# A decode layer on one core: the products with wo as a loop with addresses in registers

## The chip, the core and the metric

The kernel runs on one core of a Trainium2 chip. A core has five engines, each with its own instruction stream: TensorE (PE, matrix products; its weight loads are listed as PEld), VectorE (DVE), ScalarE (ACT), GpSimd (POOL) and SyncE (SP). [...] Engines work on SBUF, an on-chip memory of 128 partitions; TensorE writes its results to PSUM, another one. DMA engines move data between HBM and SBUF. Engines wait for each other by semaphores. The metric is the device time of one execution in microseconds.

## What is computed

One step of a decoder layer for four sequences (B = 4, D = 576): layernorm, attention over the last 4096 positions of a cache with 16 key/value heads and 32 query heads of 128, then layernorm and a gated MLP with F = 4608, each with a residual. Cut to what matters:

```python
W = min(4096, max(256, Sk // 4))
q = (x @ wq).reshape(B, Sq, Hq, Dh).transpose(0, 2, 1, 3)
k = jnp.repeat(k_cache[:, :, Sk - W:, :], rep, axis=1)
v = jnp.repeat(v_cache[:, :, Sk - W:, :], rep, axis=1)
p = softmax(einsum("bhqd,bhkd->bhqk", q, k) * Dh ** -0.5)
o = einsum("bhqk,bhkd->bhqd", p, v)
attn = o.transpose(0, 2, 1, 3).reshape(B, Sq, Hq * Dh) @ wo      # 4096 x 576
h = x + attn
hn = layernorm(h)
gate = relu(hn @ W_gate); up = hn @ W_up
out = h + (gate * up) @ W_down
```

## The kernel before

The cache is read in 16 units ("quads") of four (batch, head) pairs each, one 4 MB transfer for K and one for V per quad, into four slots of the SBUF tensor `pool`. For each quad, DVE transposes K in four pieces (`kT`, line 451), PE multiplies it with the queries (`qk`, line 544), DVE and ACT do the softmax, DVE transposes the probabilities, and PE multiplies them with V (`pv`, line 562). PE's program runs this as a hardware loop of eight turns of two quads (`S.loop`, lines 115 to 147, called at line 593); its head is placed with `head_slot`. Everything else on every engine is unrolled. No register enters an address anywhere: in the loop, registers hold only the values that semaphores are compared with (line 86, 143).

Order within an engine is the order of the code in `prog_pe`, `prog_dve`, `prog_act`, `prog_pool` and `prog_sync`. `Sched` runs these programs twice, once to number the semaphore counts of named operations and once to emit them, and puts in the waits that each operation's `deps` ask for.

After the loop, PE finishes the last quad and, with DVE, scales the attention output (`o_bf`, line 489). Four products with `spread` (line 602) bring it into the layout of `oX`, 128 partitions by EO = 32 groups by 4 sequences, which ACT copies to SBUF (line 395). Then come the products with wo (lines 604 to 610). wo lies in `pool` as 128 partitions by 32 rows of D = 576; for each row `e_`, PE loads `oX[:, e_, :]` as weights (128 x 4) and multiplies the row with it in two halves of HD = 288 columns. All 32 rows add up in the same 4 x 576 of PSUM (`attn`). The second half is a matmul with `held=True` (lines 515 to 518), which uses the weights already loaded.

The last matmul is named ATTN. What waits for it: DVE's `h_row` (line 492), which adds x and begins the second layernorm (lines 493 and 494); and all six transfers of W_down (lines 300 to 304), because they go to the place in `pool` where wo lies. These six stand on SP's queue behind those of W_gate and W_up (lines 293 to 297), which go elsewhere in `pool`, and ahead of the store of the output (line 316). SP issues every large transfer.

After the layernorm PE transposes the result (line 611), ACT copies it to `hnT`, PE forms gate and up (lines 621 to 640), ACT takes the relu, DVE multiplies (line 496) and transposes to `hhT` (line 500), and PE forms the 36 products with W_down, each in two column parts in separate PSUM partitions, `down(0)` and `down(1)` (lines 642 to 651). ACT and DVE copy these to `out_sb` (lines 406 and 503), which SP stores.

## Time and profile before

| | |
|---|---|
| runs, median (lowest to highest) | 377.74 us (377.6 to 378.22), 3 runs |
| profiled execution | 377.95 us |
| its span | 376.6 us |
| mean granted TensorE clock | 0.918 |
| HBM read | 159.58 MB, 424 GB/s over the span |
| busy: PE / DVE / ACT / POOL | 307.4 / 226.6 / 53.4 / 6.1 us |
| 64 matmuls with wo | 343.19 to 353.04 us |
| six W_down transfers | issued from 353.06, last landed at 373.32 us |
| products with W_down | 366.84 to 374.74 us |

The profile is one execution. Times in it are microseconds from the start of the span; the execution's own time is 1.35 us more than the span. Lines such as L513 are lines of the kernel; since a helper records all matmuls, L513 is a matmul that loads its weights and L515 one with held weights, and the names after them say which product it is. A name like `sc<-pool,oX` gives the tile written and the tiles read, without indices. "Idle before, releaser" tells how long the engine stood idle ahead of an instruction and what ended that; "issue" means that nothing in the profile explains the wait. The PE clock column is the share of full clock that was granted.

### The profile page before, as it was taken

To read this page: it belongs to the slowest core of one execution; us is meant where nothing else is said; L and a number is where in the kernel's file an instruction comes from. 1 tells how busy PE (TensorE), PEld (TensorE's weight loads), DVE (VectorE), ACT (ScalarE), POOL (GpSimd) and SP (SyncE) were. 2 spreads that over 40 slices of the span, in tenths; PEclk is the share of its full clock that TensorE was granted. 3 is DMA by queue.
4 is the path that set the end of the run, shared out by engine and by line. 5 is a ranking of instruction groups with operands and counts; after the bars stand their busy time and mean duration, and the time that the engine had idled before them with its cause. 6 is when DMAs were issued, how large, how long until landed. Compare 5 with 4: busy or idle time off the path is not lost.

```text
span 376.6 us, 2757 instructions
## 1 busy us (share of the span) xinstructions
PE 307.4 (82%) x1454; PEld 74.0 (20%) x778; DVE 226.6 (60%) x165; ACT 53.4 (14%) x140; POOL 6.1 (2%) x16
## 2 busy tenths in 40 slices
PE   0439999959995999599959996899679977986677
PEld 0102221212121212022201221122112211222214
DVE  8255849494839492949475758675677658222230
ACT  2231220202020202002200211021102010101020
POOL 6000000000000000000000000000000000000000
PEclk9959999989998999589976999899989998996988
DMA  8999999999999999999999999999999999999995
GB/s 335 445 444 432 404 445 445 425 412 442 442 421 421 442 445 432 407 442 445 432 411 439 445 432 414 435 445 432 414 435 445 432 418 435 433 421 435 442 399 237
DMA packets 6501, 159.66 MB, mean 424 GB/s; under 512 B 728, under 2 KB 864, under 8 KB 1632
## 3 DMA queue, kind: packets, MB, share of 16 engines
q1 hardware_dynamic: 6488, 159.59, 98.8%
q8 instruction: 3, 0.05, 0.1%
q14 instruction: 2, 0.02, 0.0%
q10 hardware_dynamic: 8, 0.00, 0.0%
HBM read 159.58 MB, written 0.00 MB: 424 GB/s over the span
## 4 chain that ended last, share of the span: by engine, by line
DMA 60%; DVE 27%; PE 11%; ACT 1%; SPq 1%; issue 0%; DVEq 0%
DMA pool<-in_A_k_cache_dram 55%; DVE kT L451 20%; DMA pool<-in_B_W_down_dram 5%; DVE acc L468 4%; PE sc L513 3%; PE sc L515 3%; DVE P L465 2%; PE val L513 2%; PE val L515 2%; PE pb L513 1%; DVE o_bf L489 0%; ACT L386 0%; DVE probT L462 0%; DVE rmx L454 0%; ACT P L386 0%
## 5 line engine op out<-in xcount | busy, mean ns | idle before, releaser
L451 DVE STREAM_TRANSPOSE kT<-pool 128x2048 f32<-128x2048 f32 x64 | 142.7, 2279 | 20.2 <-DMA pool<-in_A_k_cache_dram 20.1
L513 PE MATMUL sc<-kT,qz 128*128 128x512 bf16 x256 | 109.2, 426 | 40.3 <-DVE kT L451 40.2
L513 PE MATMUL val<-pool,probT 128*64 128x512 bf16 (+2 forms) x344 | 111.2, 374 | 3.1 <-DMA pool<-in_B_W_down_dram 3.1
L515 PE MATMUL sc<-kT,qz 128*128 128x512 bf16 x256 | 108.3, 423 | 0.0
L515 PE MATMUL val<-pool,probT 128*64 128x512 bf16 x272 | 103.1, 379 | 0.0
L513 PEld LDWEIGHTS sc<-kT,qz 128*128 128x128 bf16 x256 | 26.3, 103 | 149.5 <-DVE kT L451 77.1
L513 PEld LDWEIGHTS val<-pool,probT 128*64 128x64 bf16 (+1 forms) x344 | 34.1, 107 | 89.1 <-issue 77.6
L454 DVE TENSOR_REDUCE rmx<-sc 128x1 f32<-128x1024 f32 x16 | 19.6, 1225 | 38.5 <-PE sc L515 38.5
L381 ACT ACTIVATE diag<-spot,rmx 128x16 f32<-128x16 f32 x16 | 4.9, 307 | 242.5 <-DVE rmx L454 242.5
L462 DVE STREAM_TRANSPOSE probT<-P 128x1024 bf16<-128x1024 bf16 x16 | 19.9, 1245 | 20.5 <-ACT P L386 20.5
L386 ACT ACTIVATE P<-sc,bias 128x1024 bf16<-128x1024 f32 x16 | 17.8, 1115 | 18.7 <-DVE bias L457 18.7
L375 ACT COPY qz<-qrep 32x128 bf16<-32x128 bf16 x64 | 18.8, 293 | 0.6
L457 DVE TENSOR_REDUCE bias<-pb 128x1 f32<-128x16 f32 x16 | 2.8, 175 | 22.0 <-PE pb L513 22.0
L465 DVE TENSOR_TENSOR P<-val,mask 128x1024 f32<-128x1024 f32 x8 | 9.5, 1190 | 10.6 <-PE val L515 10.6
L468 DVE TENSOR_REDUCE acc<-P 128x128 f32<-128x1024 f32 x8 | 15.2, 1898 | 0.3
L513 PE MATMUL sc<-pool,oX 128*4 128x288 bf16 x32 | 9.4, 324 | 0.4 <-ACT oX L395 0.4
L515 PE MATMUL sc<-pool,oX 128*4 128x288 bf16 x32 | 9.4, 324 | 0.0
L525 PE MATMUL pb<-ident_b,xn_bf 4*128 4x4 bf16 (+1 forms) x5 | 0.4, 179 | 10.7 <-DVE xn_bf L419 10.7
L492 DVE TENSOR_TENSOR h_row<-sc,x_bf 4x576 f32<-4x576 f32 x1 | 0.7, 746 | 11.0 <-PE sc L515 11.0
L513 PE MATMUL sc<-col,foe 4*128 4x512 bf16 x16 | 6.3, 397 | 1.2 <-ACT qrep L361 1.2
L513 PEld LDWEIGHTS pb<-diag,same 128*128 128x128 f32 x32 | 4.8, 188 | 10.0 <-ACT diag L381 10.0
L513 PE MATMUL pb<-diag,same 128*128 128x16 f32 x32 | 6.3, 273 | 0.0
(103 smaller groups left out, 79.1 us busy)
## 6 DMA issues: line engine op xcount, KB each, us to landing
pool<-in_A_k_cache_dram SPq DMA_DIRECT2D x16, 4096.0 KB, 27.3
pool<-in_A_v_cache_dram SPq DMA_DIRECT2D x16, 4096.0 KB, 27.3
pool<-in_A_wo_dram SPq DMA_DIRECT2D x1, 4608.0 KB, 18.4
pool<-in_B_W_gate_dram SPq DMA_DIRECT2D x1, 4608.0 KB, 19.9
pool<-in_B_W_up_dram SPq DMA_DIRECT2D x1, 4608.0 KB, 23.2
pool<-in_A_wq_dram SPq DMA_DIRECT2D x1, 4096.0 KB, 12.6
pool<-in_B_W_down_dram SPq DMA_DIRECT2D x1, 2016.0 KB, 13.7
pool<-in_B_W_down_dram SPq DMA_DIRECT2D x1, 1296.0 KB, 16.5
```

The lines of the kernel that those rows point to most:

```text
L375: S.op(a, lambda e, src=src, dst=dst: e.copy(out=dst, in_=src), deps=deps, name=("QZ", i) if g == 3 else None, signal=g == 3, inc=8 if i = ...
L381: S.op(a, lambda e, i=i: e.activation(out=diag[:, i % 2, :], in_=spot[:, :], func=ACT.Copy, scale=rmx[:, i % 2:i % 2 + 1]), deps=[("RMAX", ...
L386: S.op(a, lambda e, i=i: e.activation(out=Pb[:, (i % 2) * 1024:(i % 2 + 1) * 1024], in_=sc[:, (i % 2) * 1024:(i % 2 + 1) * 1024], func=ACT ...
L451: S.op(v, lambda e: e.transpose(out=dst, in_=src), deps=deps, name=("TR", f), inc=3 if f == 5 else 1)
L454: S.op(v, lambda e: e.tensor_reduce(out=rmx[:, i % 2:i % 2 + 1], in_=sc[:, (i % 2) * 1024:(i % 2 + 1) * 1024], axis=AX.X, op=ALU.max), dep ...
L457: S.op(v, lambda e: e.tensor_reduce(out=bias[:, i % 2:i % 2 + 1], in_=pb[TPB][:, 16 * (i % 2):16 * (i % 2) + 16], axis=AX.X, op=ALU.min), ...
L462: S.op(v, lambda e: e.transpose(out=pT[i % NPT], in_=Pb[:, (i % 2) * 1024:(i % 2 + 1) * 1024]), deps=[("EXP", i)] + ([("PV", i - NPT)] if ...
L465: S.op(v, lambda e: e.tensor_tensor(out=own_sb[:, :].rearrange("p (x d) -> p x d", d=DH), in0=val[:, :].rearrange("p (x d) -> p x d", d=DH ...
L468: S.op(v, lambda e: e.tensor_reduce(out=acc[:, w, :], in_=own_sb[:, :].rearrange("p (x d) -> p d x", d=DH), axis=AX.X, op=ALU.add), deps=[ ...
L492: S.op(v, lambda e: e.tensor_tensor(out=h_row[:, :], in0=attn, in1=x_bf[:, :], op=ALU.add), deps=["ATTN", land("x")], name="H")
L513: return e.matmul(o, lhsT=l, rhs=r, start=start, stop=stop, skip_group_check=skip)
L515: return e.add_instruction(mybir.InstMatmult(name=nc.get_next_instruction_name(), start_tensor_calc=start, stop_tensor_calc=stop, bass_ski ...
```

## The change

Rows 1 to 30 of the products with wo become a hardware loop on TensorE of ten turns of three rows. The row's number follows from the loop's counter, and the address of the weights in `oX` and the address of the row in `pool` are computed from it in registers (`bass.ds` with a register as its start). Row 0, which carries the waits, and row 31, which signals ATTN, stay outside with fixed addresses. A new function `Sched.repeat` makes the loop; unlike `Sched.loop` it gives no `head_slot`, and no wait in it depends on the counter. The products, their order and their places are the same. The other engines' programs are the same.

```diff
+    def repeat(self, eng, n, body):
+        if not self.emit:
+            for i in range(n):
+                body(i)
+            return
+        count = self.counters[eng]
+        with self.engines[eng].Fori(0, n) as i:
+            body(i)
+        assert self.counters[eng] == count
...
-            for e_ in range(EO):
-                deps = [land(("wo",)), "OX"] if e_ == 0 else []
+            def wo_row(e_, first, last):
+                deps = [land(("wo",)), "OX"] if first else []
                 for u in range(2):
-                    c0 = at[("wo",)] + e_ * D + u * HD
-                    mm(attn[:, u * HD:(u + 1) * HD], oX[:, e_, :], pool[:, c0:c0 + HD], e_ == 0, e_ == EO - 1,
-                       deps=deps, name="ATTN" if e_ == EO - 1 and u == 1 else None, held=u == 1)
+                    mm(attn[:, u * HD:(u + 1) * HD], oXf[:, bass.ds(e_ * B, B)], pool[:, bass.ds(e_ * D + at[("wo",)] + u * HD, HD)], first, last,
+                       deps=deps, name="ATTN" if last and u == 1 else None, held=u == 1)
                     deps = []
+
+            oXf = oX[:, :, :].rearrange("p e b -> p (e b)")
+            wo_row(0, True, False)
+            S.repeat(t, (EO - 2) // 3, lambda i: [wo_row(i * 3 + 1 + k, False, False) for k in range(3)])
+            wo_row(EO - 1, False, True)
```

In the built kernel a turn of this loop holds, on PE: seven fused register instructions (33 register operations), three single register additions, one compare-and-branch, three weight loads and six matmuls.

## The prediction

> **What bounds the kernel now.** I read the chain of waits first, over the last 25 us, because the change touches only work that lies there. Columns are start, duration, what.

> ```profile
> 352.90 0.14 PE sc L515
> 353.04 0.02 issue
> 353.06 0.33 SPq L303
> ...
> 354.38 18.94 DMA pool<-in_B_W_down_dram
> 373.32 0.04 issue
> 373.36 0.70 PE val L513 x7
> ...
> 374.78 0.42 DVE out_sb L503
> ```

> The last product with wo ends at 353.04. Two things wait for it: SP, which then issues the six W_down transfers (L303), and DVE's h_row (L492), behind which stand the second layernorm, the gate and up products, and the products with W_down. The chain goes by the transfers, but the other branch is close behind. Next come the stages, by busy time in windows (length, then busy time and count by engine, TensorE clock, DMA share, GB/s).

> ```profile
> 343.00:347.00 4.00, 3.81 (x17) 1.10 (x9) 0.00 (x0) 1.32 (x2) 0.00 (x0) 0.50 0.96 409
> 347.00:353.10 6.10, 6.03 (x49) 1.96 (x23) 0.04 (x1) 0.00 (x0) 0.00 (x0) 1.00 1.12 481
> 361.00:366.80 5.80, 3.36 (x71) 0.61 (x24) 2.68 (x5) 2.06 (x3) 0.00 (x0) 1.00 0.98 410
> 366.80:374.80 8.00, 7.30 (x72) 4.32 (x72) 0.27 (x2) 0.02 (x1) 0.00 (x0) 0.79 0.73 299
> ```

> In the wo stage (the first two rows) PE is busy without a gap, first at half clock, then at full. In the last row it is busy for 7.30 of 8.00 us while W_down still arrives: the down stage waits for data now and then, and has little room. Third, the timeline of one wo row, late in the stage:

> ```profile
> 352.50 0.09 PEld L513 LDWEIGHTS sc<-pool,oX 128*4 128x4 bf16 x1 [0.16 <-issue]
> 352.62 0.29 PE L513 MATMUL sc<-pool,oX 128*4 128x288 bf16 x1
> 352.74 0.29 PE L515 MATMUL sc<-pool,oX 128*4 128x288 bf16 x1
> ```

> A row costs 0.24 us at full clock (two starts 0.12 apart), 0.48 at half. Last, TensorE's sequencer, in the records of the lines that make its first loop and its waits (count: shortest/median/longest ns, first and last start):

> ```profile
> L139 PEldq MOVE  x9: 37/37/39, 20.2 to 285.5; - x9
> L139 PEldq COMPARE_BRANCH  x9: 76/208/309, 20.3 to 323.4; - x9
> L139 PEldq ALU_OP  x8: 32/32/32, 53.8 to 323.3; - x8
> L86 PEldq ALU_OP  x88: 32/32/42, 20.7 to 318.8; - x88
> ```

> **The change, part by part.** Rows 0 and 31 stay as they are. Removed are the 90 plain instructions of rows 1 to 30 (a weight load and two matmuls each), which PE executed in about 9.1 us and which cost the sequencer nearly nothing. In their place the built kernel's order of instructions has one turn, run ten times, of: seven fused register instructions holding 33 register operations in all, two single additions, the counter's addition, a compare-and-branch, three weight loads and six matmuls that take an address from a register. No wait, transfer or buffer changes on any engine.

> Now the turn, in the sequencer:
> - three single additions x 97 ns = 0.29 us;
> - the back-edge, 0.27 us;
> - seven fused instructions. The trace has none. From below, each costs at least one ALU_OP: 7 x 97 = 0.68. From above, its 33 operations cost as much as apart: 33 x 97 = 3.20. The nearest row is the ALU_OP, 32 ns of it work and 65 around it; if the 65 are paid once per instruction, 7 x 65 + 33 x 32 ns = 1.51. I take the middle of 0.68 and 1.51, 1.10;
> - nine loads and matmuls with an address in a register. From below, like the matmul with a wait on a register: 15 ns each, 0.14 (as low as 0.07 if that matmul is no dearer than 8 ns, the 120 ns from MOVE to ALU_OP less 97, over three). From above, like a DMA issue on SP with its addresses (L303, 432 ns median): 3.9. I take 97 ns, 0.87, since fetching a register is what an ALU_OP does.

> Turn T = 0.29 + 0.27 + 1.10 + 0.87 = 2.53 us. PE's own work in it is 0.73 us at full and 1.44 at half clock, so it is covered by the sequencer: the engine waits for its instructions. [...]

> The stage: row 0 starts at 343.19 as before, while the sequencer goes on to MOVE and the entry branch (0.47 us, under row 0's 0.48), so the first turn starts at 343.65. Ten turns, less 0.17 for the last branch, plus 0.54 for row 31 (352.50 to 353.04): the stage ends at 344.0 + 10T = 369.3, which is 16.3 later than 353.04.

> What that delays. SP's queue holds the six W_down issues behind this one wait, then only the output's store. The earlier wg and wu transfers land by about 361.8 (issued at 337.26 and 337.74, 23.2 and 24.1 us to landing), so the DMA engines then idle until about 369.4. The 5.3 MB that follow take some 12.7 us at 410 GB/s, plus some 2 us to start: all landed by about 384. The other branch, h_row to hhT, is a fixed string of DVE, ACT and PE work and moves as a whole: the down products, whose hhT was ready by the semaphore wait at 366.43 and which began at 366.84 only when the first W_down piece came, may begin at 366.5 + 16.3 = 382.8, long after that piece. So W_down, now ending the chain, no longer does; hhT does.

> That gives a little back. A down row's matmuls start 136 ns apart at full clock and 267 at half. With the 3.41 us of half clock that this stage had, 36 rows without waits take 12.8 x 0.267 + 23.2 x 0.136 + 0.3 for the end = 6.9 us: from 366.5 to 373.4, where the trace ends at 374.74. So -1.3 us (-3.0 if all at full clock, +1.7 if all at half).

> Sum against the profiled execution, 377.95 (span 376.6): 377.95 + 16.3 - 1.3 = **392.9 us**; for any turn, 367.6 + 10T. The median of the runs is 377.74, 0.2 below the profiled one, less than what is uncertain here.

> **Rivals.**
> - Cheap addresses: a matmul with a register's address passes like the one with a register's wait. T = 0.29 + 0.27 + 1.10 + 0.14 = 1.80, 385.6; with every bound low, 1.31, 380.7. For it: 15 matmuls and loads in 15 ns. Against: there the register held a wait, not an address.
> - Dear register operations: 33 x 97 ns. T = 0.29 + 0.27 + 3.20 + 0.87 = 4.63, 413.9 (with addresses as dear as a DMA issue instead, T = 5.55, 423.1). Against: they are fused into seven instructions.
> - Not slower: the sequencer's work hides under PE's. This needs 10T below 9.0 + 1.3, so T below 1.03, or ten register instructions at 76 ns or less. It decides only if fused instructions cost about what ALU_OP's busy time says (32 ns): T = 10 x 0.032 + 0.27 + 0.07 = 0.66, all hidden, some 377.7. Against it: no register operation in PE's sequencer is followed by its next control instruction in less than 96 ns.
> - The code is fetched anew at each back-edge. The instruction queue's 16 KB packets took 1.0 to 1.1 us each; nine of them add at least 9.9: 402.8. Against: seven taken back-edges of a body eleven times as long took 207 to 233 ns. [...]
> - The clock stays at half after a loop of sparse matmuls, in place of the mix of before: the up stage's 2.6 us of matmuls double, and the down stage goes to +1.7. That is 2.6 + 3.0 us on top: 398.5. Against: the K loop of before, whose PE also waits, is mostly at full clock.

> **How the numbers follow.** The forecast (388 to 398.5, the clock's rival at its edge) gets 0.51, cheap addresses (380.5 to 388) 0.25, dear register operations or addresses (398.5 and above) 0.15, refetching 0.04, not slower 0.05. The range 382 to 405 leaves out not slower, the lowest bounds of cheap addresses (0.04), and the upper half of the dear case (0.08). A change of 0.2% (0.76 us) can be told from none; not slower splits into same 0.03 and faster 0.02, the other cases are slower, 0.95.

> **What would show it.** In the changed kernel PE has idle time ended by issue in the wo stage, some 1.1 to 1.8 us a turn, and the sequencer's records follow each other without a gap: fused ones at about 160 ns of pitch, matmuls at about 97 each. The stage ends near 369. DMA has an idle stretch from 362 to about 370, and the chain at the end goes by PE and DVE from the stage to the output, with no W_down transfer. Wrong would be: turns of under 1.03 us, wo matmuls still back to back, or a W_down transfer still in the chain.

## The result, and the profile after

The changed kernel takes 382.92 us (median of 4 runs, 381.82 to 383.84) against 377.86 (4 runs, 377.6 to 378.22): a ratio of 1.0132, 95% interval 1.0104 to 1.0161. It is slower, by 5.1 us where 15 were forecast, and 382.92 lies in the range, at its low edge. The profiled execution took 382.82 us with a span of 381.5.

Where the time went, from the two traces (us):

| | before | after | later by |
|---|---|---|---|
| first matmul with wo | 343.19 | 343.75 | 0.57 |
| last matmul with wo ends | 353.03 | 359.47 | 6.44 |
| the wo stage | 9.84 | 15.72 | 5.88 |
| first half of hhT ready | 366.39 | 372.76 | 6.37 |
| products with W_down begin | 366.84 | 372.91 | 6.06 |
| products with W_down end | 374.74 | 379.63 | 4.89 |
| span | 376.6 | 381.5 | 4.9 |

The first 0.57 us come from ahead of the change, in work that is the same in both kernels (see e2 and e3 on what moves it); the stage itself grew by 5.88, the string of work behind it moved along, and the last stage gave some of it back. The chain of waits over the end of the changed kernel (start, duration, what):

```profile
359.35 0.14 PE sc L525
359.48 0.02 issue
359.51 0.76 DVE h_row L502
...
361.87 0.58 DVE hn_row L429
...
368.17 0.28 PE pb L523 x4
...
371.98 0.79 DVE probT L510
372.77 0.14 issue
372.90 6.75 PE val L523 x46
379.65 0.02 issue
379.68 0.42 DVE out_sb L513
```

No transfer is left in it. The products with W_down start 0.14 us after DVE's transpose to hhT and run without a break; SP's issues of W_down, now at 359.5, are no part of it. Busy time in windows (length; busy time and count of PE, PEld, DVE, ACT, POOL; PE clock; DMA share; GB/s), for the wo stage, the stretch to hhT and the products with W_down, first of the kernel before, then of the changed one:

```profile
343.10:353.10 10.00, 9.84 (x64) 3.05 (x32) 0.04 (x1) 1.24 (x1) 0.00 (x0) 0.81 1.06 453
353.10:366.80 13.70, 8.06 (x130) 1.91 (x50) 5.11 (x11) 3.10 (x8) 0.00 (x0) 0.88 0.95 402
366.80:374.80 8.00, 7.30 (x72) 4.32 (x72) 0.27 (x2) 0.02 (x1) 0.00 (x0) 0.79 0.73 299
```

```profile
343.70:359.50 15.80, 13.70 (x64) 2.60 (x32) 0.00 (x0) 1.21 (x1) 0.00 (x0) 0.81 0.96 412
359.50:372.90 13.40, 7.99 (x130) 1.83 (x51) 4.87 (x11) 3.10 (x8) 0.00 (x0) 0.87 0.97 391
372.90:379.70 6.80, 6.72 (x72) 4.04 (x72) 0.54 (x2) 0.03 (x1) 0.00 (x0) 0.75 0.15 53
```

In the first row of the changed kernel PE is idle for 2.1 us, and its busy time is padded by matmuls that no longer overlap: 13.70 us for the 64 matmuls that took 9.84 before, though one is as long as then (282 to 448 ns against 286 to 444). In the last the DMA share is 0.15, against 0.73 before: nearly all of W_down is there when the products start, and its last transfer, landing at 375.90, is ahead of the rows that need it. Now one turn of the loop at full clock, in the timeline:

```profile
351.84 0.08 PEld L523 LDWEIGHTS sc<-pool,oX 128*4 x1 [0.69 <-issue]
351.85 0.28 PE L523 MATMUL sc<-pool,oX 128*4 x1 [0.33 <-issue]
351.98 0.28 PE L525 MATMUL sc<-pool,oX 128*4 x1
352.19 0.08 PEld L523 LDWEIGHTS sc<-pool,oX 128*4 x1 [0.27 <-issue]
352.22 0.28 PE L523 MATMUL sc<-pool,oX 128*4 x1
352.35 0.28 PE L525 MATMUL sc<-pool,oX 128*4 x1
352.60 0.08 PEld L523 LDWEIGHTS sc<-pool,oX 128*4 x1 [0.33 <-issue]
352.63 0.28 PE L523 MATMUL sc<-pool,oX 128*4 x1
352.76 0.28 PE L525 MATMUL sc<-pool,oX 128*4 x1
```

Rows start 0.37 to 0.41 us apart in place of 0.24, the next turn 1.53 us later, and what ends PE's idle time is "issue": no engine and no transfer that the profile shows. What fills these stretches are the records of PE's own sequencer, which the trace lists under PEldq: in the changed kernel 70 FUSED_REGOPS (the fused register instructions), 126 ALU_OP (the single ones), 19 COMPARE_BRANCH and 10 MOVE, and no such record for any other engine. By line (count: shortest/median/longest ns, first and last start):

```profile
L121 PEldq FUSED_REGOPS  x10: 78/78/83, 344.0 to 357.7; - x10
L121 PEldq ALU_OP  x10: 32/32/32, 345.1 to 358.8; - x10
L121 PEldq COMPARE_BRANCH  x10: 76/212/214, 345.2 to 358.9; - x10
...
L528 PEldq FUSED_REGOPS  x30: 55/55/60, 344.2 to 358.7; - x30
...
L523 PEldq FUSED_REGOPS  x30: 51/79/79, 344.1 to 358.5; - x30
L523 PEldq ALU_OP  x20: 32/34/36, 344.5 to 358.6; - x20
```

From the starts in the trace: a fused instruction of 6 operations (78 or 79 ns busy) holds the sequencer for 137 ns, one of 4 (55 or 60) for 113 to 118. The one of 3 (51) is always followed by a weight load and a matmul here and takes 129 with them; alone, in e2 below, it takes 109. Worked out from the 109 and 137 ns for 3 and 6 operations, an estimate is some 81 ns for the instruction and 9.3 for each operation; it gives 118 for 4. Between the fused instruction at 350.339 and the next at 350.457, 118 ns, stands a held matmul with its address in a register: beside the estimated 118 it adds nothing that shows. A weight load with its matmul adds some 20 ns in most turns. Nor is that a price for each: in e6 all nine weight loads and matmuls of a turn stand behind its fused instruction of 3 operations, and this one takes 129 ns again, so the nine together add 20, and at most 70 in the longer of e6's turns. A back-edge takes 271 ns from the branch to the first fused instruction of the next turn.

### The profile page after: what moved, and what is told of

Read it like the earlier page. It is cut to its first block, busy times and chain, and to the rows that moved or that the text cites. A ratio compares the mean times of both kernels' runs of the same rounds, so it can differ in the third digit from the quotient of the medians.

```text
span 381.5 us, 2868 instructions
## 1 busy us (share of the span) xinstructions
PE 311.4 (82%) x1454; PEld 73.3 (19%) x778; DVE 226.9 (59%) x165; ACT 53.4 (14%) x140; POOL 6.1 (2%) x16
## 4 chain that ended last, share of the span: by engine, by line
DMA 54%; DVE 27%; PE 16%; issue 1%; ACT 1%; SPq 0%; DVEq 0%
DMA pool<-in_A_k_cache_dram 54%; DVE kT L461 18%; PE sc L523 5%; PE sc L525 4%; DVE acc L478 4%; PE val L523 4%; DVE P L475 2%; PE val L525 2%; PE pb L523 1%; DVE o_bf L499 0%; ACT L396 0%; DVE probT L472 0%; DVE rmx L464 0%; ACT P L396 0%; PE pb L525 0%
## 5 line engine op out<-in xcount | busy, mean ns | idle before, releaser
L461 DVE STREAM_TRANSPOSE kT<-pool 128x2048 f32<-128x2048 f32 x64 | 142.7, 2279 | 20.4 <-DMA pool<-in_A_k_cache_dram 20.2
L523 PE MATMUL sc<-pool,oX 128*4 (+1 forms) x32 | 10.8, 337 | 2.5 <-issue 2.0
L525 PE MATMUL sc<-pool,oX 128*4 (+1 forms) x32 | 10.9, 341 | 0.0
```

Source lines behind the costliest of these rows:

```text
L461: S.op(v, lambda e: e.transpose(out=dst, in_=src), deps=deps, name=("TR", f), inc=3 if f == 5 else 1)
L523: return e.matmul(o, lhsT=l, rhs=r, start=start, stop=stop, skip_group_check=skip)
L525: return e.add_instruction(mybir.InstMatmult(name=nc.get_next_instruction_name(), start_tensor_calc=start, stop_tensor_calc=stop, bass_ski ...
```

## The experiments

Theory A: the sequencer's register instructions set the pace of the wo stage, and any delay of the stage beyond a little room at the end delays the end. Against it stand, for the pace, the loop itself (B) and the instructions with an address in a register (C); for the end, that W_down goes on setting it (E), or that the loss is in PE's sparse pace (F).

| kernel | turn, us | wo stage, us | median, us | ratio to before, 95% |
|---|---|---|---|---|
| before | none | 9.84 | 377.76 to 377.87 | 1 |
| changed | 1.53 | 15.72 | 382.92 | 1.0104 to 1.0161 |
| a2, changed again | 1.53 | 15.71 | 382.75 | 1.0110 to 1.0139 |
| e1, fixed addresses | 0.73 (PE) | 10.47 | 377.81 | 0.9995 to 1.0020 |
| e2, wo's address only | 1.15 | 11.92 | 380.09 | 1.0042 to 1.0095 |
| e3, weights' address only | 1.16 | 11.95 | 379.03 | 1.0017 to 1.0044 |
| e4, two turns of fifteen | 6.05 | 12.56 | 379.47 | 1.0029 to 1.0060 |
| e5, plain, more rows | none | 16.12 | 382.80 | 1.0102 to 1.0144 |
| e6, addresses together | 1.03 to 1.08 | 11.42 | 377.98 | 1.0001 to 1.0019 |
| e7, six rows a turn | 1.61 to 1.95 | 11.49 | 378.00 | 0.9992 to 1.0011 |

**e1: the loop without registers in addresses.**

```diff
-            S.repeat(t, (EO - 2) // 3, lambda i: [wo_row(i * 3 + 1 + k, False, False) for k in range(3)])
+            S.repeat(t, (EO - 2) // 3, lambda i: [wo_row(1 + k, False, False) for k in range(3)])
```

> The same loop of ten turns, but with the addresses of rows 1 to 3 in every turn, so no register enters an address (rows 4 to 30 are left out of the result, the number of products is the same). Theory A (the sequencer's register work sets the pace): a turn needs 0.10 (counter) + 0.27 (back-edge) us of the sequencer plus some 0.06 for loads and matmuls, less than the 0.73 that PE needs, so the wo stage takes its 9.85 us as in the kernel before and the time is 377.9 +- 0.5. Theory B (the loop itself costs: each back-edge lets PE run dry, or fetches code anew): an idle stretch of 0.3 us or more per turn stays, 379 or more.

377.81 us, not to be told from before. In e1's trace the matmuls follow each other as if unrolled (minimum/median/maximum ns, first and last start):

```profile
L523 PE MATMUL sc<-pool,oX x32: 286/286/448, 344.1 to 354.1; 128*4 128x288 bf16 x32
L525 PE MATMUL sc<-pool,oX x32: 286/286/448, 344.3 to 354.2; 128*4 128x288 bf16 x32
```

The first back-edges come 0.38 us apart, ahead of PE's work, and the later ones once per 0.73 us of it (1.44 at half clock). The stage is 0.6 us longer than before because more of it fell into the half clock, 5.1 us in place of 3.8. So in e1 the back-edges are hidden, 0.38 us of the sequencer under 0.73 of PE. Nor does a fetch of code show: the instruction queue moved no packet during the stage, in e1 or in the changed kernel (there the nearest ones start at 331.42 and 372.29 us, and the stage lasts from 343.75 to 359.47). B falls.

**e2 and e3: one address at a time.** `w_` is a second row number; e2 gives the loop's row to wo and a fixed one to the weights, e3 the reverse.

```diff
-                    mm(..., oXf[:, bass.ds(e_ * B, B)], pool[:, bass.ds(e_ * D + at[("wo",)] + u * HD, HD)], first, last,
+                    mm(..., oXf[:, bass.ds(w_ * B, B)], pool[:, bass.ds(e_ * D + at[("wo",)] + u * HD, HD)], first, last,
...
# e2
+            S.repeat(t, (EO - 2) // 3, lambda i: [wo_row(i * 3 + 1 + k, False, False, 1 + k) for k in range(3)])
# e3
+            S.repeat(t, (EO - 2) // 3, lambda i: [wo_row(1 + k, False, False, i * 3 + 1 + k) for k in range(3)])
```

> The loop with only the address of the wo row in a register; the weights are those of rows 1 to 3 in every turn (left out: the other rows' weights). Six fused instructions with 6, 3, 4, 3, 4, 3 operations and no single ones but the counter. Theory A, with the pitches of the changed kernel's trace (137, 109 and 118 ns for 6, 3 and 4 operations): turn 0.70 + 0.10 + 0.27 + 0.06 = 1.13 us, 378.9 by 367.6 + 10T, up to 380 where PE at half clock needs 1.44 for a turn. Theory C (what costs is a matmul or load that takes its address from a register, here six of nine): 2/3 of the changed kernel's loss, 381.2.

> The loop with only the address of the weights in a register; the wo rows are 1 to 3 in every turn (left out: the other rows). Three fused instructions with 6, 4, 4 operations and three single additions besides the counter. Theory A: 0.137 + 2 x 0.118 + 4 x 0.097 + 0.27 + 0.06 = 1.09 us a turn, 378.5, up to 380 with the half clock; about the same as with wo alone. Theory C: three of nine instructions have an address in a register, 1/3 of the loss, 379.5, and 1.7 us less than with wo alone.

The turns took 1.15 and 1.16 us, where A said 1.13 and 1.09, and the stages 11.92 and 11.95. With six instructions that take a register's address against three, C wanted the stages apart; they are equal. The times are 1.1 us apart all the same, where C asked for 1.7, and e2's 380.09 is above A's 378.9 to 380. But that is not by way of this stage: in the profile of e2 it began at 344.68, in that of e3 at 343.76. The work ahead of it is the same in both, and the clock that it was granted is not. These are the last products with K, in windows as above, e2 first, then e3:

```profile
316.00:318.60 2.60, 2.60 (x8) 0.43 (x3) 2.60 (x2) 0.00 (x0) 0.00 (x0) 0.50 0.97 416
318.60:320.20 1.60, 1.60 (x5) 0.29 (x2) 0.04 (x1) 0.00 (x0) 0.00 (x0) 0.50 0.81 348
```

```profile
316.00:318.60 2.60, 2.60 (x9) 0.48 (x4) 2.60 (x2) 0.00 (x0) 0.00 (x0) 0.66 1.05 454
318.60:320.20 1.60, 1.60 (x9) 0.29 (x3) 0.10 (x1) 0.00 (x0) 0.00 (x0) 1.00 0.81 348
```

At a clock of 0.50 in place of 1.00 between 318.6 and 320.2, the last product with K ended at 322.66 in e2 and at 321.53 in e3. This accounts for the later start in these two executions; for the medians it is not shown, so the verdict rests on the turns.

**e4: fewer back-edges.**

```diff
-            S.repeat(t, (EO - 2) // 3, lambda i: [wo_row(i * 3 + 1 + k, False, False) for k in range(3)])
+            S.repeat(t, (EO - 2) // 15, lambda i: [wo_row(i * 15 + 1 + k, False, False) for k in range(15)])
```

> The changed kernel with two turns of fifteen rows, same result. The addresses and their arithmetic stay, eight of nine taken back-edges go, each 0.10 + 0.27 us. Theory A: 30 rows at 0.137 + 0.097 + 0.118 + 0.02 = 0.37 us and one back-edge, 11.5 us, 379.1, up to 380.4 with the half clock. Theory C: as the changed kernel, 382 to 383. If the sequencer did not set the pace at all, also 382 to 383.

379.47 us, with every address still in a register. A turn took 6.05 us; where PE is at full clock the sequencer's records repeat every 0.37 us per row, as expected. Eight back-edges fewer at 0.37 are 2.9 us; the stage is 3.2 shorter than the changed kernel's. C, which asked for 382 to 383, falls here too. The stage is 1.1 us longer than the 11.5 expected, a figure for full clock: its first 4.3 us were at half clock, where PE needs 0.48 us for a row.

**e5: the delay without the loop.**

```diff
-            for e_ in range(EO):
+            for e_ in [0] + [r for r in range(1, 27) for _ in range(2)] + [27, 28, 29, 30, 31]:
```

> The kernel before, unrolled and with fixed addresses, but with rows 1 to 26 of wo multiplied twice (the result counts them double): 26 x 0.244 = 6.3 us of plain work ahead of the last product, the delay of the changed kernel (5.9) without its loop. Theory D (any delay of this stage moves the string of work from h_row to hhT, which then sets the end; W_down, which ended the chain, gives back some 1.4 us): 377.9 + 6.3 - 1.4 = 382.8 +- 1.2, no W_down transfer in the chain at the end. Rival E (the end goes on being set by W_down, whose transfers queue behind W_up's until 361.8 anyhow): 378 to 379.5. Rival F (the loss is in the sparse pace and its effect on PE's clock, not in the delay): under 381.

382.80 us. A plain stage of 16.12 us costs what the loop's 15.72 costs, and the chain at the end of e5 is the changed kernel's:

```profile
372.09 0.79 DVE probT L500
372.88 0.14 issue
373.01 6.75 PE val L513 x46
379.76 0.02 issue
379.79 0.42 DVE out_sb L503
```

D holds, E and F fall: what matters in this stage is how late its last product ends, not what fills the time.

**e6 and e7: the same loop with less register work.** The addresses of a turn are lowered together at its head, and the counter steps by 4 per row, so that wo's offset is 144 times the counter and the weights' offset is the counter itself. The held matmul names fixed weights, which it does not load.

```diff
...
+                    for k in range(n):
+                        aps.append([e.lower_ap(pool[:, bass.ds(j * 144 + k * D + at[("wo",)], HD)]),
+                                    e.lower_ap(oXf[:, bass.ds(j + B * k, B)]),
+                                    e.lower_ap(pool[:, bass.ds(j * 144 + k * D + at[("wo",)] + HD, HD)])])
+                    for r0, l0, r1 in aps:
...
+            S.repeat_from(t, B, B * (EO - 1 - NR) + 1, B * NR, lambda j: rows(j, NR))
```

> The changed kernel, same result and ten turns of three rows with both addresses in registers, but the addresses of a turn are worked out together at its head, with a counter that steps by 12 so that both offsets are multiples of it, and none for held weights: five fused instructions with 6, 6, 6, 6, 3 operations and no single ones but the counter. Theory A: 4 x 0.137 + 0.109 + 0.097 + 0.27 + 0.06 = 1.09 us a turn in place of 1.53, a stage of some 11.7 us and 378.5 to 379.2. Theory C (what costs is an instruction with an address in a register): as the changed kernel, 382 to 383.

> As the one before, with five turns of six rows: nine fused instructions of 6 operations a turn. Theory A: 9 x 0.137 + 0.097 + 0.27 + 0.13 = 1.73 us for six rows, which need 1.46 of PE at full clock and 2.88 at half; five turns take 8.6 us of the sequencer against 9.1 that 30 rows took before, so nearly all is hidden: 377.9 to 378.4, not to be told from the kernel before or barely. Nothing here can be faster than before, since W_down's transfers then set the end again.

Five fused instructions a turn in place of seven fused and two single, and the loss is all but gone: 377.98 us. e6's turn is 1.03 to 1.08 us, just about the 1.03 that the prediction gave as the point below which the loop costs nothing. The chain at the end of e6:

```profile
368.67 0.79 DVE probT L518
369.46 0.14 issue
369.60 5.07 PE val L531 x48
374.67 0.02 issue
374.69 0.41 DVE out_sb L521
```

The string to hhT still sets the end here: the last product with wo ended at 356.14, 3.1 us later than before, half of it because the stage began later (344.72). But the products with W_down ran at full clock throughout and took 5.07 us, so this execution ended as early as before; with the changed kernel's 6.7 us it would have ended 1.7 us later. The median is half a microsecond better than expected. That the clock is the reason for it is argued from this one trace, and not shown.

e7, with six rows a turn, is not to be told from before. Its trace does not show the loop wholly hidden, though. The shortest turn took 1.61 us where PE needs 1.46 at full clock, and the stage took 11.49 us, about as in e6; of the 1.65 more than before some 1.2 are half clock (6.3 us of it in the stage in place of 3.8). The chain at the end goes by hhT, where W_down's transfers were expected. Here too the products with W_down ran at full clock, in 5.13 us. No version beat the kernel before: in that one W_down's transfers set the end, and none of these edits brings them earlier.

**a2: the changed kernel once more.**

> The changed kernel unaltered, beside the three others on the same chip: 382 to 384, a turn of 1.53 us.

382.75 us, turns of 1.53, a stage of 15.71.

## Why the prediction was right and wrong

The mechanism was right: the engine waits for its sequencer, the loop is slower, the end passes from W_down's transfers to hhT. The sum's own formula, 367.6 + 10T, gives 382.9 for the measured turn of 1.53 us, and the profiled execution took 382.82. That it fits to 0.1 us is partly luck, as two of the bullets below show. What was wrong is the size of T, 2.53 where 1.53 was measured, and with it every time that hangs on it. Of the 1.00 us between them, the instructions with an address in a register make some 0.77 and the fused ones 0.24.

- **Loads and matmuls with an address in a register, 97 ns each, 0.87 us: the step that failed.** All nine together took some 0.1 us of the turn: 1.53 less 0.27 and 0.29 for back-edge and single additions and less 0.86 for the fused ones. The reason given, that fetching a register is what an ALU_OP does, doesn't hold: the nearest row was the other one, a matmul that waits for a register's value and passes within 15 ns, which the prediction had in hand and used as the lower end. e2 against e3 shows the same: twice as many such instructions, an equal turn (1.15 and 1.16 us).
- **Fused register instructions, 1.10 us.** They took 0.86 by their pitches, inside 0.68 to 1.51. The upper of these bounds took 32 ns for each operation, where the estimate from the measured pitches is 9.3.
- **Single additions and back-edge, 0.29 and 0.27 us.** As predicted from the first loop's records: 97 and 271 ns.
- **Entry of the loop.** 0.47 us were allowed, for MOVE and a taken branch as at the first loop. Here the trace has MOVE at 343.867 and the loop's first instruction at 343.965, 98 ns and no branch. So the first turn began 0.21 us after row 0 instead of 0.46. As the sequencer sets the pace of all ten turns, this brought the end of the stage some 0.25 us forward, and hid part of the 0.57 by which the stage began late, which the formula doesn't have.
- **The stage and what hangs on it.** 16.3 us of delay became 6.4, of which 5.9 by the change and 0.6 from ahead of it. With that, W_down is issued from 359.50, when W_up is still arriving (until 362.15), so the idle stretch of the DMA engines from 362 on did not appear. (The 5.3 MB of W_down at 410 GB/s are 12.9 us and not 12.7, which changes nothing.) The step "hhT now ends the chain" held regardless, and e5 shows it for a delay of plain work.
- **The give-back, -1.3 us.** h_row moved by 6.44 us, the end by 4.9: -1.5. Of these the earlier start of the products with W_down gives 0.4 and their running without waits 1.2 (7.89 to 6.72 us), with 3.41 us of half clock in both, as assumed. That these fell on the products with W_down again was luck: in the profiles of e4, e6 and e7 none did.
- **The rivals.** Cheap addresses was the case that came true, as 1.53 lies between its 1.31 and 1.80; it had 0.25 where the likeliest had 0.51. Dear register operations and refetching are excluded by the records of the turn (0.86 us for the 33 operations, where 3.20 were feared) and by e1 (377.81 us). (Nine packets of 1.0 to 1.1 us would have been 9.0 to 9.9 us, not at least 9.9.) Not slower was put below T = 1.03; e6, with 1.03 to 1.08, lost 0.2 us and e3, with 1.16, lost 1.2, which fits, but no run shows where the limit is. The clock's rival fell: the windows above have 0.81, 0.87 and 0.75 of full clock for the changed kernel against 0.81, 0.88 and 0.79 before.
- **The signs.** PE idle by issue, as foretold: yes, but some 0.8 us a turn at full clock (1.53 less 0.73) and 0.1 at half, not 1.1 to 1.8; the profile, which counts each spaced matmul whole, shows 0.33 of it as idle. Fused pitch "about 160 ns": 109 to 137. Matmuls "about 97 each": no, nine in some 0.1 us. No W_down transfer in the chain: yes. The end of the stage near 369: 359.5.

## What to carry to other kernels

In this kernel the loop on TensorE cost nothing where its sequencer needed less time for a turn than the engine did (e1: 0.38 against 0.73 us). So count the register instructions of a turn, not the instructions that use the registers. Here each fused one cost 110 to 140 ns, a back-edge 370 with the counter, and a matmul with its address in a register nothing that shows (113 to 118 ns from a fused instruction of 4 operations to the next record with a held matmul between, by the estimate 118 without); working out the addresses of a turn together brought the price from 5 us to 0.2 (e6), and longer turns besides to none that can be told (e7), with what is said there of the clock. And a stage that isn't named in the chain of waits can have very little room: here the other branch, by the prediction's estimate 1.3 us behind, took over.

## What the runs showed of the hardware

In the changed kernel and in e6, where the string of PE work sets the end, the granted clock shows in the time of the last stage. In the traces of the kernel before and of the changed one the half clock comes in stretches of 3.41, 6.83 or 10.24 us (in the changed kernel from 342.73 for 6.83 us, and from 373.45 for 3.41), and where they fall differs between these executions (in the one before from 340.14 for 6.83 us, and from 367.45 for 3.41): the products with W_down took 6.72 us in the changed kernel with one such stretch in them and 5.05 us in e6 with none. The spread of the runs does not settle whether this is all: those of the changed kernel lie within 2.0 us and those of e5 within 2.6 (381.0 to 383.59), those of the kernel before, beside the changed one, within 0.6; but its 23 runs beside e5 lie within 1.9 and those of e1 within 2.1, though W_down's transfers set the end in the profiles of both kernels.
